# Two 256-column tiles in place of one 512-column tile, and other due times for the DMA transposes, in a planned attention and feed-forward kernel

## The chip, the core and the metric

The kernel runs on one core of a Trainium2 chip. A core has TensorE (PE, matrix multiplication into the PSUM banks), VectorE (DVE), ScalarE (ACT), GpSimd (POOL) and SyncE (SP, which here only issues DMAs), each with its own queue of instructions, and 16 DMA engines between HBM and the on-chip memory SBUF. The metric is the device time of one execution in microseconds. Smaller is better.

## What is computed

A decayed linear attention over 4 batches, 8 heads, 768 positions and 64 dimensions, in blocks of 64 positions, followed by a feed-forward layer with the gate h * cos(h):

```
for b in range(nb):
    intra = np.einsum('bhic,bhjc->bhij', qb, kb) * Dmask[None]
    intra = np.einsum('bhij,bhjd->bhid', intra, vb)
    inter = np.einsum('bhid,bhde->bhie', qb * lam_pow[None], kv_state)
    out[:, :, sl] = intra + inter
    kb_dec = kb * rev_pow[None]
    kv_state = lam_block[None, :, None, None] * kv_state + np.einsum('bhsd,bhse->bhde', kb_dec, vb)
...
x = attn_out.transpose(0, 2, 1, 3).reshape(B * S, H * D)      # 3072 x 512
h = x @ w_in                                                  # 3072 x 2048
g = h * np.cos(h)
return g @ w_out                                              # 3072 x 512
```

## The kernel before

**Blocks, pairs and tiles.** The 3072 rows are 24 blocks of 128 rows, numbered in the order in which they are worked. Two neighbouring blocks are a pair, one from each of two batches, and pair 2 to pair 11 go through `prepare`, `add_scores` and `add_stretch` (pairs 0 and 1, the lead-in, have their own code in `add_span`). The feed-forward layer works on tiles of blocks: the list `TILES` (line 21) says how many blocks each tile has, and `add_ffn(i)` emits the work of tile i. A tile of 4 blocks has 512 columns and holds two pairs, a tile of 2 blocks has 256 columns and holds one.

**One pair of attention.** SP loads q, k and v (line 253). GpSimd scales and casts them (lines 329, 333, 337). From pair 3 on, two DMA transposes issued by SP (line 365) make `qkT` from `qk`; pair 2 is transposed on TensorE. TensorE then does the scores (`ps_s`, line 407) and the update of the running state (`ps_kv`, line 419), and for the pair before the values (`ps_o`, line 470) and the carried part (line 502). VectorE masks the scores (line 412) and adds up the state (line 425), ScalarE casts the state (line 430) and the attention's output into `xT` (line 510), which is the input of the feed-forward layer. Most of the time the values of pair p, the scores and update of pair p+1 and the carried part of pair p stand together in TensorE's queue, as one group of 128 small matmuls.

**One tile of feed-forward.** For each of 16 hidden steps f, TensorE does four matmuls as wide as the tile into a PSUM bank `ps_h` (line 732), ScalarE takes the cosine (line 738) and VectorE multiplies it with `ps_h` into `g` (line 744), which frees the bank. For each block of the tile, 16 matmuls of 512 columns (line 779, in four quarters of four) make `ps_f`; ScalarE copies it to SBUF as `o_sb` (line 793), and SP stores it (lines 800 and 802).

**What sets the order.** The order of each engine's queue is made ahead of time by a small list scheduler, `Planner.order` (lines 74 to 117): each task has an engine, a duration, dependencies and a priority, PSUM banks and buffers are counted, and whichever task can start first on an engine goes next, ties by priority. The priorities of attention and of projections come from the tile lists `unit` and `begins` (lines 234 and 235), which come from `TILES`. `T_LAT` (line 28) tells the planner, for each pair, how many microseconds after the DMA transpose its result counts as there (line 372); a pair without an entry has 1.2. The planner's times only make the order; on the chip the engines wait on semaphores. `HELD` (line 29) makes the stores of the first twelve blocks wait until the transposes of pair 10 have been issued (line 808); their outputs lie in 12 buffers `o_held` until then, the later ones in 3 buffers `o_sb`. `ALONE` (line 27) names the pairs whose scores stand alone.

**Buffers that tie one pair or tile to another.** Eight PSUM banks in all. Three buffers each of `qk` and `qkT`, six of `v_s` (three pairs), two of `xT` and two of `g`: the attention of tile i writes the `xT` that the hidden steps of tile i-2 have read, and the gates of tile i write the `g` that the projections of tile i-2 have read.

Of the kernel before, what the change touches and what calls it, by code (L numbers as in the profile page):

```python
# [17 lines left out]

SPANS = 2
DMA_FROM = 6  # L20
TILES = [4, 2, 2, 2, 2, 4, 4, 4]
SPLIT = 5
BANKS = 8
LAG = 2
ATT = 0.95
LOAD_US = 1.22
ALONE = [3, 4]
T_LAT = {3: 2.46, 4: 4.62, 5: 3.15, 6: 4.42, 7: 3.9, 8: 3.84, 9: 6.24, 10: 5.52, 11: 4.89}
HELD = (10,) * 12

APART = [3, 11]
# [115 lines left out]
def kernel(  # L147
# [19 lines left out]
    KF = D_FF // P  # L167
    assert sum(TILES) == NBLK
    first = [sum(TILES[:i]) for i in range(len(TILES) + 1)]

# [62 lines left out]

    unit = [MM(n * P, 4 * KF) + MM(DM, KF * n) + ATT * n for n in TILES]
    begins = [sum(unit[:i]) for i in range(len(unit) + 1)]

    def prio_attn(n, part):
        i = next(i for i in range(len(TILES)) if n < first[i + 1])
        return begins[i - 1] + unit[i - 1] * (n - n % 2 - first[i] + 2 * part) / TILES[i]

# [71 lines left out]
    def tile_of(n):  # L312
        return next((i, n - first[i]) for i in range(len(TILES)) if n < first[i + 1])

    def prepare(pr):
# [51 lines left out]
        for i, src in enumerate((a, k_)):  # L367
            get = None if i else "qkT"
            if 2 * pr >= DMA_FROM:
                head, T[pr, i] = dma("SP", 1.4, 1.3, partial(transposes_dma, i=i), 2 * pr + i - LAG + 1.5,  # L370
                                     src + ([qkT_head[pr]] if i else []), get=get, ordered=False)
                T[pr, i].lat = T_LAT.get(pr, 1.2)
                if i and 2 * pr + LAG < NBLK:
# [563 lines left out]
```

## Time and profile before

| what | value |
|---|---|
| median of 3 runs | 202.32 us (202.25 to 202.38) |
| the profiled execution's own time | 202.32 us |
| its span, first to last instruction | 200.6 us |
| granted TensorE clock in every stretch | 1.00 |
| ps_h, 128x512, 236 matmuls | mean 379 ns of one |
| ps_h, 128x256, 296 matmuls | mean 273 ns of one |
| ps_f, 128x512, 368 matmuls | mean 379 ns of one |
| cosine on ScalarE, 128x512 and 128x256 | 687 and 478 ns |
| gate on VectorE, 128x512 and 128x256 | 690 and 423 ns |
| weight load for ps_h | 98 ns |
| mask of scores, sum of state on VectorE | 684 and 680 ns |
| copy of ps_f to SBUF on ScalarE | 587 ns |
| DMA transpose, issue to landing | 2.9 to 6.3 us, median 4.4 |

The duration of one matmul in the table includes its way through the array, and the next one starts before it ends; what a matmul takes of TensorE's time is the distance from its start to the next start. TensorE's work from about 14 us to 198 us of the span is the stretch that the change lies in: lead-in up to 43 us, then ten pairs of attention among seven tiles of feed-forward, and the closing projections.

### The profile page before, as it was taken

What the parts mean: (1) busy time and instruction counts of PE and PEld (TensorE: products, weight loads), DVE (VectorE), ACT (ScalarE), POOL (GpSimd) and SP (SyncE); (2) the same over time, 40 slices, a digit from 0 to 9 for tenths busy, and PEclk for the clock granted to TensorE, in tenths of its full rate; (3) what the DMA queues carried; (4) which work ended last, traced back from release to release, by engine and by line L of the source; (5) the groups of instructions that cost most, each with busy time, mean ns of one, the idle gap of its engine ahead of it and who ended that gap; (6) DMA issues with size and microseconds to landing.
All of it is one profiled execution on the core that took longest, in us unless ns stands there. A gap on an engine that the chain in (4) does not pass through costs nothing.

```text
span 200.6 us, 5756 instructions
## 1 busy us (share of the span) xinstructions
PE 195.4 (97%) x2407; PEld 110.2 (55%) x2407; DVE 111.8 (56%) x211; ACT 116.3 (58%) x221; POOL 64.7 (32%) x85
## 2 busy tenths in 40 slices
PE   8799999999999999999999999999999999999994
PEld 2467444547758647867655454544445444444443
DVE  2978772258957816966735679367445454444001
ACT  5878771139768636948654878377455564345120
POOL 5793003066462636372736364003700000000000
DMA  5999999989997999999999899898921010111112
GB/s 161 305 191 204 203 199 215 174 197 227 218 213 172 198 222 199 216 204 187 220 192 242 154 226 178 232 394 197 260 83 51 6 52 3 52 52 52 52 56 105
DMA packets 96620, 33.93 MB, mean 169 GB/s; under 512 B 84690, under 2 KB 93650, under 8 KB 96594
## 3 DMA queue, kind: packets, MB, share of 16 engines
q1 hardware_dynamic: 89088, 28.78, 65.1%
q0 software_dynamic: 7360, 4.72, 16.5%
q8 instruction: 19, 0.31, 0.6%
q10 hardware_dynamic: 146, 0.07, 0.1%
q14 instruction: 7, 0.06, 0.1%
HBM read 27.26 MB, written 6.29 MB: 167 GB/s over the span
## 4 chain that ended last, share of the span: by engine, by line
PE 85%; DMA 9%; SPq 2%; DVE 1%; POOL 1%; ACT 0%; issue 0%; POOLq 0%
PE ps_h L732 41%; PE ps_f L779 36%; DMA v_f<-in_v_dram 4%; DMA sp_f<-in_k_dram 3%; SPq L253 2%; DMA k_f<-in_k_dram 2%; PE ps_o L470 2%; PE ps_o L502 2%; PE ps_kv L419 1%; PE ps_s L407 1%; PE ps_o L638 1%; PE ps_kv L625 1%; POOL k_sp L593 1%; DVE v_s L337 0%; PE ps_t L601 0%
## 5 line engine op out<-in xcount | busy, mean ns | idle before, releaser
L744 DVE TENSOR_TENSOR g<-ps_h,cos 128x256 bf16<-128x256 f32 (+1 forms) x133 | 70.4, 542 | 39.5 <-ACT cos L738 38.3
L779 PE MATMUL ps_f<-w_out_sb,g 128*128 128x512 bf16 (+2 forms) x400 | 90.5, 371 | 0.0
L732 PE MATMUL ps_h<-xT,w_in_sb 128*128 128x256 bf16 (+1 forms) x532 | 89.5, 320 | 0.0
L738 ACT ACTIVATE cos<-ps_h,halfpi 128x256 f32<-128x256 f32 (+1 forms) x133 | 72.1, 571 | 27.6 <-PE ps_h L732 26.3
L732 PEld LDWEIGHTS <-w_in_sb 128*128 128x128 bf16 x532 | 51.5, 98 | 32.9 <-DVE xT L510 0.4
L779 PEld LDWEIGHTS <-g 128*128 128x128 bf16 x400 | 37.5, 98 | 40.4
L329 POOL TENSOR_TENSOR qk<-q_f,q_scale 128x512 bf16<-128x512 f32 x19 | 19.5, 1045 | 38.1 <-DMA q_f<-in_q_dram 31.5
L793 ACT COPY o_sb<-ps_f 128x512 f32<-128x512 f32 (+1 forms) x24 | 13.8, 573 | 24.5 <-PE ps_f L779 24.4
L337 POOL TENSOR_TENSOR v_s<-v_f,v_scale 128x512 bf16<-128x512 f32 x19 | 19.7, 1044 | 10.5 <-DMA v_f<-in_v_dram 10.1
L510 ACT CAST xT<-ps_o 128x512 bf16<-128x512 f32 x15 | 8.1, 588 | 11.5 <-PE ps_o L502 9.1
L412 DVE TENSOR_TENSOR s_m<-ps_s,mask 128x512 bf16<-128x512 f32 x20 | 12.9, 684 | 3.3 <-PE ps_s L407 2.8
L333 POOL CAST qk<-k_f 128x512 bf16<-128x512 f32 x18 | 11.1, 614 | 6.2 <-DMA k_f<-in_k_dram 6.1
L425 DVE TENSOR_TENSOR sum<-sum,ps_kv 128x512 f32<-128x512 f32 x15 | 10.2, 680 | 0.6
L430 ACT CAST S<-sum 128x512 bf16<-128x512 f32 x15 | 9.1, 616 | 2.3 <-DVE sum L425 2.2
L487 DVE COPY spare<-ps_o 1x1 f32<-1x1 f32 x8 | 1.2, 156 | 15.3 <-PE ps_o L470 15.3
L253 POOL DMA_DIRECT2D w_out_sb<-in_moe_w_out_dram x4 | 3.0, 776 | 15.8 <-DMA q_f<-in_q_dram 15.8
L793 DVE COPY o_sb<-ps_f 128x384 f32<-128x384 f32 x1 | 0.6, 556 | 11.5 <-PE ps_f L779 11.5
L470 PEld LDWEIGHTS <-v_s 64*64 64x64 bf16 x320 | 4.2, 106 | 4.6 <-issue 3.2
L470 PE MATMUL ps_o<-s_m,v_s 64*64 64x64 bf16 x288 | 5.9, 197 | 0.1
L617 DVE TENSOR_TENSOR s_m_sp<-ps_s,mask_sp 128x512 bf16<-128x512 f32 x8 | 5.1, 682 | 1.3 <-PE ps_s L612 1.3
L864 PE MATMUL ps_idle<-const-float32-1.0 128*128 128x512 f32 (+1 forms) x6 | 4.8, 893 | 0.8 <-PEq L921 0.8
L502 PE MATMUL ps_o<-qkT,S 64*64 64x64 bf16 x304 | 5.1, 195 | 0.0
(75 smaller groups left out, 83.6 us busy)
## 6 DMA issues: line engine op xcount, KB each, us to landing
q_f<-in_q_dram SPq DMA_DIRECT2D x20, 256.0 KB, 3.8
k_f<-in_k_dram SPq DMA_DIRECT2D x20, 256.0 KB, 4.5
v_f<-in_v_dram SPq DMA_DIRECT2D x20, 256.0 KB, 4.8
out_dram<-o_sb SPq DMA_DIRECT2D x19, 256.0 KB, 2.8
w_out_sb<-in_moe_w_out_dram POOLq DMA_DIRECT2D x4, 512.0 KB, 12.4
sp_f<-in_q_dram SPq DMA_DIRECT2D x2, 512.0 KB, 5.0
sp_f<-in_k_dram SPq DMA_DIRECT2D x2, 512.0 KB, 5.5
w_in_sb<-in_moe_w_in_dram POOLq DMA_DIRECT2D x2, 512.0 KB, 8.8
```

Source lines behind the costliest of these rows:

```text
L329: vec[e].tensor_mul(new_qk()[:, 0, :, s], live.pop(("q_f", 2 * pr + s)), q_scale[:, c, :].unsqueeze(2).to_broadcast([P, H, D]))
L333: (nc.scalar.copy if early else nc.gpsimd.tensor_copy)(new_qk()[:, 1, :, s], live.pop(("k_f", 2 * pr + s)))
L337: vec[e].tensor_mul(live["v_s", 2 * pr + s], live.pop(("v_f", 2 * pr + s)), v_scale[:, c, :].unsqueeze(2).to_broadcast([P, H, D]))
L412: nc.vector.tensor_mul(t, live["s", pr][s], mask.unsqueeze(1).to_broadcast([P, H, D]))
L425: nc.vector.tensor_add(new, live["sum", pr, 0] if half else live["sum", pr - 1, 1], live["kv", pr][half])
L470: yield lambda h=h: nc.tensor.matmul(o[halves[h % 2], h // 2], lhsT=live["v_s", n0 + s][m, h, :], rhs=live["s_m", n0 + s][m, h, :], start= ...
L502: nc.tensor.matmul(live["o", n0 + s][halves[h % 2], h // 2, halves[half]], lhsT=S[r, h, :], rhs=live["qkT", pr][r, 0, h, halves[half]], st ...
L732: nc.tensor.matmul(t[:, :n], lhsT=w_in_sb[:, kd, f * P:(f + 1) * P], rhs=live["xT", i][:, kd, at], start=(kd == 0), stop=(kd == KD - 1))
L738: nc.scalar.activation(c[:, :n], live["h", i, f, at.start][:, :n], AF.Sin, bias=halfpi)
L744: return nc.vector.tensor_mul(live["g", i][:, f, at], live.pop(("h", i, f, at.start))[:, :n], live.pop(("c", i, f, at.start))[:, :n])
L779: nc.tensor.matmul(live["f", i, j, piece][:, :width], lhsT=live["g", i][:, f, j * P:(j + 1) * P], rhs=w_out_sb[:, f, part], start=(f == 0) ...
L793: (nc.scalar.copy if eng == "ACT" else nc.vector.tensor_copy)(o[:, :width], live["f", i, j, piece][:, :width])
```

## The change

Two lists of constants change, and with them the order that the planner makes:

```diff
-TILES = [4, 2, 2, 2, 2, 4, 4, 4]
+TILES = [4, 2, 2, 2, 2, 2, 2, 4, 4]
...
-T_LAT = {3: 2.46, 4: 4.62, 5: 3.15, 6: 4.42, 7: 3.9, 8: 3.84, 9: 6.24, 10: 5.52, 11: 4.89}
+T_LAT = {3: 2.6, 4: 5.0, 5: 3.15, 6: 5.8, 7: 5.52, 8: 7.8, 9: 6.8, 10: 6.0, 11: 5.3}
```

Pairs 6 and 7, blocks 12 to 15, were one tile of four blocks and are two tiles of two. The planner now takes the results of the DMA transposes as there later, for all pairs but 3 (0.14 us later) and 5 (the same) by 0.4 to 4.0 us. No other line differs.

What follows for the instructions: the hidden steps of pairs 6 and 7 are 2 x 16 steps of four 256-column matmuls, with as many cosines and gates, in place of 16 steps of four 512-column matmuls. Around the end of tile 2 and from there on, TensorE's queue has attention and feed-forward in another order:

```
before (matmuls in order, from the hidden steps of tile 1 on)
ps_h 64 | scores 3, update 3 | ps_f 16 | values 3, carried 3 | ps_f 8 | ps_h 48 | ps_f 4 | scores 4, update 4 | ...
after
ps_h 64 | ps_f 4 | scores 3, update 3 | ps_f 16 | values 3, carried 3 | ps_f 12 | ps_h 44 | scores 4, update 4 | ...
```

The groups with the values of pairs 7 and 9 had projections right behind them, that of pair 8 hidden steps of 512 columns. Now each of the three has 256-column hidden steps right behind it: after the group of pair 7, two hidden steps, a quarter projection, two hidden steps, a quarter projection, and so on; after the groups of pairs 8 and 9, one hidden step, a quarter projection, two hidden steps. In the queues of ScalarE and VectorE the cosines, gates, casts and copies follow the same order. GpSimd's queue is unchanged. In SP's queue the stores of blocks 4 to 13 (before: 4 to 12) stand between the transposes of pair 10 and the loads of pair 11, and the store of block 14 stands between the two transposes of pair 11 (before: the store of block 13 stood ahead of both).

## The prediction

> **What bounds the kernel now.** I read the page's shares and slices first, then TensorE's own waits, then the chain that ended last in order of time, and last the timelines around one attention group and of SP's queue.
>
> ```profile
> span 200.6 us, 5756 instructions
> ...
> PE 195.4 (97%) x2407; PEld 110.2 (55%) x2407; DVE 111.8 (56%) x211; ACT 116.3 (58%) x221; POOL 64.7 (32%) x85
> ...
> PE   8799999999999999999999999999999999999994
> ```
>
> TensorE is busy 97% of the span and every slice but the first two and the last is full. The page warns that such a share is modelled, so the waits are needed too. TensorE's list of waits for other engines is short, and all of it lies in the lead-in:
>
> ```profile
> PE ps_idle L864 <- PEq L921: 0.8, 1, 0.8
> PE ps_t L601 <- DVE q_sp L593: 0.5, 1, 0.5
> PE ps_t L601 <- DVE k_sp L593: 0.3, 1, 0.3
> PE ps_t L601 <- POOL k_sp L593: 0.3, 1, 0.3
> ```
>
> The chain in order of time (start us, us, what) tells whether the matmuls follow each other at their own pitch:
>
> ```profile
> 46.36 7.02 PE ps_h L732 x64
> ...
> 77.85 6.99 PE ps_h L732 x64
> ...
> 109.76 9.50 PE ps_h L732 x44
> ...
> 120.24 0.45 PE ps_o L502 x32
> 120.69 4.42 PE ps_h L732 x20
> ...
> 183.89 13.87 PE ps_f L779 x80
> ```
>
> The first two rows are 64 matmuls of 256 columns: 7.02/64 = 109.7 ns and 6.99/64 = 109.2 ns each. The third is of 512 columns: 9.50/44 = 215.9 ns. The last is the closing projection without a break. I went through the start of every ps_h and ps_f matmul from 14.3 us on: apart from the step to another kind of matmul (0.09 us, once at each attention group), the one start that is late is at 42.8 us, by about 0.18 us, for v_s of pair 2. So from 43 us to the last matmul the order of TensorE's queue costs nothing but its work.
>
> **The change part by part.** The order of instructions of the two kernels differs on TensorE only after the 64 ps_h of tile 1, at 53.3 us of this trace; the lead-in, the 0.18 us and all of POOL's order are the same.
>
> *The split tile.* Pairs 6 and 7 were one tile of 512 columns; now each is a tile of 256. 16 hidden steps x 4 = 64 matmuls of 512 columns go, 128 of 256 columns come. 64 x (2 x 109.2 - 215.9) ns = 64 x 2.5 = +0.16 us on TensorE, in the path. With 109.7 it is 64 x 3.5 = +0.22; with the medians of start to start in the trace (109 and 216) it is 64 x 2 = +0.13. I take 0.16, the row of the undisturbed run of tile 3. The 64 more weight loads of 98 ns (6.3 us of weight-load time) lie under matmuls: in those same runs each 98 ns load is already hidden inside a 109 ns pitch; uncovered they would be up to 6.3 us, but 282 pairs of such matmuls in this trace keep a mean of 109.3 ns.
>
> The projections (ps_f) stay 128 wide in their weights and 512 in columns: none added. Attention groups stay: 11 stretches of small matmuls from 53 us on, in both orders, so the 0.09 us steps stay, 0.
>
> [...]
>
> *Cosine and gate.* By the page's groups of one form each, ScalarE does 32 cosines of 478 ns for 16 of 687 (+4.3 us) and VectorE 32 gates of 423 ns for 16 of 690 (+2.5 us), spread over the about 30 us in which pairs 6 and 7 are worked. ScalarE is busy 13.2 of the 20 us from 100 to 120 us and VectorE 11.2, and TensorE covers it: 0. In a run of hidden steps TensorE takes 4 x 109 = 437 ns for each; 14 cosines in a row took 5.71 us, 408 ns each, so ScalarE keeps up.
>
> *The due times (T_LAT) and the moved attention.* They only shift where attention stands among the feed-forward matmuls. Summing pitches over the new order from 53.31 us, the scores of pairs 3 to 11, at 53.3, 66.2, 74.9, 86.6, 96.3, 106.7, 119.3, 129.5 and 153.4 us now, come at about 54.2, 66.6, 74.9, 88.4, 98.1, 111.0, 121.6, 130.1 and 155.3. The trace has the second transpose of each pair landed at 52.2, 62.7, 72.3, 82.7, 93.7, 103.5, 114.1, 125.1 and 146.6. The least margin rises from 1.1 us (pair 3) to 2.0; none shrinks. Later attention frees qkT, qk and v_s later; three pairs of each are held, and the tightest, the transpose of pair 10 issued at 118.9, needs carried values of pair 7, which end at about 112.3. Loads are not delayed: 0.
>
> *SP's queue.* One more store (block 13) goes ahead of pair 11's loads, and one store (block 14) between its two transposes.
>
> ```profile
> 122.08 6.04 SPq L800 DMA_DIRECT2D out_dram<-o_sb  x8
> 128.21 5.72 SPq L802 DMA_DIRECT2D out_dram<-o_sb  x9
> 133.99 1.35 SPq L253 DMA_DIRECT2D q_f<-in_q_dram  x2
> ...
> 141.73 2.75 SPq L365 DMA_TRANSPOSE qkT<-qk  x2
> ```
>
> A store's issue is 5.72/9 = 0.64 us. Block 13's projection ends at about 132.7 in the new order, its copy (0.59 us) at about 133.6, before SP comes to it at 134.0; so pair 11's loads start 0.6 us later. Block 14's copy is done at about 143.1; SP waits there under 1 us with the transpose of k, and then only stores, behind it. It lands by about 148.5; the scores that want it come at 155.3. Cover: 6.8 us; 0.
>
> Sum: +0.16 us, bounds +0.13 and +0.22 without a stall. Span 200.6 + 0.16 = 200.8 us. The profiled execution's own time is 202.32, the same as the median of the three runs, with 1.7 us around the span; so 202.32 + 0.16 = **202.48 us**. Under 0.2% (0.40 us), about what a measurement of this kernel can tell from no change.
>
> **The rivals.**
>
> *Bank waits after the moved attention: slower, 203.2 us.* In the new order the groups of pairs 7/8, 8/9 and 9/10 are followed at once by 256-column hidden steps, which ask for a PSUM bank every 0.44 us, where the group at 119.25 us asks every 0.86. Each group takes 6 of 8 banks and VectorE frees four of them with two masks (684 ns) and two sums (680 ns). For it: the group's VectorE work ends late, here 5.4 us after its start:
>
> ```profile
> 119.18 0.32 PE L470 MATMUL ps_o<-s_m,v_s 64*64 64x64 bf16 x16
> ...
> 120.95 1.28 DVE L412 TENSOR_TENSOR s_m<-ps_s,mask 128x512 bf16<-128x512 f32 x2
> ...
> 122.15 0.68 DVE L425 TENSOR_TENSOR sum<-sum,ps_kv 128x512 f32<-128x512 f32 x1
> ```
>
> Against it: in spite of that, the chain shows 20 ps_h right behind at 4.42 us (221 ns each, the 0.09 us step in it), and the new order puts one or two hidden steps, then 0.86 us of projection, then two. Where VectorE starts the masks 0.66 us into a group, as at 86.49 us (87.15), the first bank is free at 1.35 us, just as the group's 1.34 us end, and the second at 1.95 against a need at 1.78 when no other bank is free. One group then costs between nothing and a mask, 0.68 us. One mask late at one group: 202.48 + 0.68 = 203.16; at all three, 204.5. It decides from a total of 0.24 us on.
>
> *Pair 11 late through SP: slower, 203.0 us.* It needs the 6.8 us of cover gone. The longest landing of a transpose here is 6.3 us against the median of 4.4, which takes 1.9 of it. The store ahead of the transpose of k would have to wait 5 us longer than worked out, a whole half of a block's projections and hidden steps; each microsecond beyond is one of TensorE's, and 0.5 of it gives 203.0.
>
> *The new order closes gaps: faster, down to 201.5.* For it speaks only the step at attention groups: were it hidden at all 11 (11 x 0.09 = 1.0 us), 202.48 - 1.0 = 201.5. Against it: the groups are as many, and the step stands at every one of them whatever its neighbours; other gaps there are none behind 53 us.
>
> *The change does nothing.* The orders differ, so only a cancelling gain could make it so; its time, 202.3, lies in the same 0.2%.
>
> **How the numbers follow.** Forecast, no stall, 202.40 to 202.60: 0.70. Bank waits: 0.22, of which 0.02 stay under 0.24 us. Pair 11: 0.04. Gaps closed: 0.04. So faster 0.04, same 0.70 + 0.02 = 0.72, slower 0.20 + 0.04 = 0.24. Range: from 202.30, the forecast's lower bound of 202.45 less the runs' own spread (202.25 to 202.38), to 203.20, one mask late; what lies beyond is several masks late and the gain.
>
> **What would show it.** TensorE's list of waits should again hold the lead-in alone; 128x256 ps_h should rise by 128 and 128x512 fall by 64, at 109 and 216 ns a start; 32 cosines more of 128x256. Scores of pair 8 near 111 us. A ps_h that waits for VectorE's masks or sums between 111 and 133 us would show the first rival; scores of pair 11 behind a transpose that lands after 155 the second. What would make it wrong is VectorE behind by more than one mask at those groups.

## The result, and the profile after

The changed kernel is slower. Its median is 203.46 us (202.75 to 205.34, 22 runs), that of the kernel before beside it 202.37 us (22 runs): a ratio of 1.0055, interval 1.0036 to 1.0074, so 0.55% or 1.1 us. The forecast was 202.48 us, no measurable change, with a range up to 203.20. The profiled execution took 203.63 us, with a span of 201.9 us (before: 202.32 and 200.6); the granted clock is 1.00 throughout.

The page of the changed kernel, shares of the span and the line on the instruction queue that will matter below (packets, MB, share of 16 engines):

```profile
span 201.9 us, 5935 instructions
...
PE 196.7 (97%) x2471; PEld 117.0 (58%) x2471; DVE 114.2 (57%) x227; ACT 118.4 (59%) x237; POOL 64.9 (32%) x85
...
q8 instruction: 19, 0.31, 0.6%
```

The reader is to see that TensorE has its 64 more matmuls (2471 for 2407), VectorE and ScalarE 16 more instructions each, and that TensorE is still busy for 97%. Busy time rose by 1.3 us, but the page's busy time is modelled; the waits say more. TensorE's list of waits in the changed kernel (us in total, times, longest):

```profile
PE ps_idle L864 <- PEq L921: 0.8, 1, 0.8
PE ps_h L732 <- issue: 0.8, 1, 0.8
PE ps_s L612 <- ACT kT_sp L604: 0.3, 1, 0.3
PE ps_t L601 <- DVE q_sp L593: 0.2, 1, 0.2
```

Three of the four rows are the lead-in, as before. The second is new: one matmul of ps_h is 0.8 us late, and its releaser is "issue", the profile's word for no releaser at all. Behind the lead-in no row names VectorE, a PSUM bank or a DMA. The chain in order of time (start us, us, what) shows where it is:

```profile
46.29 7.02 PE ps_h L732 x64
...
77.78 6.99 PE ps_h L732 x64
...
110.99 0.25 PE ps_o L470 x16
111.24 0.26 PE ps_s L407 x32
111.50 0.32 PE ps_kv L419 x32
111.82 0.16 PE ps_o L470 x16
111.98 0.35 PE ps_o L502 x32
112.32 0.98 PE ps_h L732 x8
113.30 0.86 PE ps_f L779 x4
114.17 0.77 PE ps_h L732 x7
114.93 0.79 issue
115.72 0.27 PE ps_h L732
115.99 0.86 PE ps_f L779 x4
...
185.16 13.87 PE ps_f L779 x80
```

The rows of 64 matmuls have the pitch of before (7.02 and 6.99 us), and so has the closing projection (13.87). The group of pairs 7 and 8 stands at 111 us and has its two hidden steps right behind it, eight matmuls, a quarter projection, and then seven matmuls of eight: between the seventh and the eighth, the last of one accumulation, 0.79 us pass. From start to start it is 1065 ns, where 109 is the pitch. The timeline of the changed kernel around it (start us, us, engine, line, operation, tiles, shape, and in brackets the idle time before it):

```profile
111.58 1.29 DVE L412 TENSOR_TENSOR s_m<-ps_s,mask 128x512 bf16<-128x512 f32 x2
...
112.25 1.05 PE L732 MATMUL ps_h<-xT,w_in_sb 128*128 128x256 bf16 x8
...
112.79 1.47 DVE L425 TENSOR_TENSOR sum<-sum,ps_kv 128x512 f32<-128x512 f32 x2
...
113.37 2.85 SPq L253 DMA_DIRECT2D v_f<-in_v_dram  x2
...
114.00 0.93 PE L732 MATMUL ps_h<-xT,w_in_sb 128*128 128x256 bf16 x7
...
115.72 0.27 PE L732 MATMUL ps_h<-xT,w_in_sb 128*128 128x256 bf16 x1 [0.79 <-issue]
115.72 0.64 PEld L779 LDWEIGHTS <-g 128*128 128x128 bf16 x4 [0.97 <-issue]
```

VectorE's masks and sums behind the group are over at 114.26 us and none of the matmuls waited for them. The eighth matmul uses the same bank as the three before it, an `xT` whose casts ended at 100.37 us, and weights of which the last load was issued at 13.8 us (the longest of them took 9.9 us to land). Weight loads and matmuls stop together, for 0.97 and 0.79 us, both down to "issue": it is TensorE's queue of instructions itself that stands still.

**What the span's 1.3 us are made of** (201.9 less 200.6, to the tenth of the page; 1.36 from the start of tile 1's hidden steps to the end, 155.60 for 154.24, and -0.07 in front of it): the pitch of the split tile, 128 x 109.3 - 64 x 215.9 ns = +0.17; the hole, 1065 - 109 ns = +0.96; the eleven attention groups, +0.22 in all (11.94 for 11.72 us, from the first small matmul of each to the next wide one; single starts in them are some 0.1 us late). That makes 1.35 of the 1.36.

### The profile page after: what moved, and what is told of

The parts are those of the page before. It is cut to its first block, busy times and chain, and to the rows that moved or that the text cites. A ratio compares the mean times of both kernels' runs of the same rounds, so it can differ in the third digit from the quotient of the medians.

```text
span 201.9 us, 5935 instructions
## 1 busy us (share of the span) xinstructions
PE 196.7 (97%) x2471; PEld 117.0 (58%) x2471; DVE 114.2 (57%) x227; ACT 118.4 (59%) x237; POOL 64.9 (32%) x85
## 4 chain that ended last, share of the span: by engine, by line
PE 90%; DMA 6%; SPq 1%; POOL 1%; issue 1%; ACT 0%; POOLq 0%
PE ps_f L779 42%; PE ps_h L732 41%; DMA sp_f<-in_k_dram 3%; DMA w_in_sb<-in_moe_w_in_dram 3%; PE ps_o L470 2%; PE ps_o L502 2%; PE ps_kv L419 1%; PE ps_s L407 1%; SPq L253 1%; POOL k_sp L593 1%; PE ps_t L359 0%; PE ps_kv L697 0%; PE ps_x L470 0%; ACT o_sb L793 0%; POOLq L593 0%
## 5 line engine op out<-in xcount | busy, mean ns | idle before, releaser
L744 DVE TENSOR_TENSOR g<-ps_h,cos 128x256 bf16<-128x256 f32 (+1 forms) x149 | 72.5, 501 | 44.0 <-ACT cos L738 42.8
L738 ACT ACTIVATE cos<-ps_h,halfpi 128x256 f32<-128x256 f32 (+1 forms) x149 | 75.3, 540 | 29.6 <-PE ps_h L732 29.3
L732 PE MATMUL ps_h<-xT,w_in_sb 128*128 128x256 bf16 (+1 forms) x596 | 91.2, 303 | 0.9 <-issue 0.8
L779 PE MATMUL ps_f<-w_out_sb,g 128*128 128x512 bf16 (+2 forms) x400 | 91.5, 371 | 0.0
L732 PEld LDWEIGHTS <-w_in_sb 128*128 128x128 bf16 x596 | 57.6, 98 | 30.1 <-DMA w_in_sb<-in_moe_w_in_dram 0.5
L329 POOL TENSOR_TENSOR qk<-q_f,q_scale 128x512 bf16<-128x512 f32 x19 | 20.0, 1065 | 43.8 <-DMA q_f<-in_q_dram 43.8
L793 ACT COPY o_sb<-ps_f 128x512 f32<-128x512 f32 (+1 forms) x24 | 13.8, 573 | 26.0 <-PE ps_f L779 26.0
```

What stands on the lines that cost most here:

```text
L329: vec[e].tensor_mul(new_qk()[:, 0, :, s], live.pop(("q_f", 2 * pr + s)), q_scale[:, c, :].unsqueeze(2).to_broadcast([P, H, D]))
L732: nc.tensor.matmul(t[:, :n], lhsT=w_in_sb[:, kd, f * P:(f + 1) * P], rhs=live["xT", i][:, kd, at], start=(kd == 0), stop=(kd == KD - 1))
L738: nc.scalar.activation(c[:, :n], live["h", i, f, at.start][:, :n], AF.Sin, bias=halfpi)
L744: return nc.vector.tensor_mul(live["g", i][:, f, at], live.pop(("h", i, f, at.start))[:, :n], live.pop(("c", i, f, at.start))[:, :n])
L779: nc.tensor.matmul(live["f", i, j, piece][:, :width], lhsT=live["g", i][:, f, j * P:(j + 1) * P], rhs=w_out_sb[:, f, part], start=(f == 0) ...
L793: (nc.scalar.copy if eng == "ACT" else nc.vector.tensor_copy)(o[:, :width], live["f", i, j, piece][:, :width])
```

## The experiments

**Theories.** *Instruction fetch:* TensorE's instructions come in blocks by DMA, and in the new order TensorE reaches the end of a block before the next one is there. For it: the hole has no releaser; the packets of the instruction queue number 19 in both kernels, of 16 KB each (16384 bytes in both traces), and TensorE's some 4,950 instructions (2471 matmuls and as many weight loads) are 19 blocks of about 256. In the order of the program the late matmul is the 3254th instruction. (TensorE's records in the trace, waits included, make it the 3266th; in every profile below that has a late start at a numbered instruction, the two counts differ by the same 12.) *Rival:* a wait on data, a bank or a due time after the moved attention, wherever the instructions lie.

### The two halves of the change, each alone

```diff
 e1_tiles_only          (after, with the due times of before)
-T_LAT = {3: 2.6, 4: 5.0, 5: 3.15, 6: 5.8, 7: 5.52, 8: 7.8, 9: 6.8, 10: 6.0, 11: 5.3}
+T_LAT = {3: 2.46, 4: 4.62, 5: 3.15, 6: 4.42, 7: 3.9, 8: 3.84, 9: 6.24, 10: 5.52, 11: 4.89}
 e2_due_times_only      (after, with the tiles of before)
-TILES = [4, 2, 2, 2, 2, 2, 2, 4, 4]
+TILES = [4, 2, 2, 2, 2, 4, 4, 4]
```

> The changed list of tiles with the due times of before. Theory F (fetch): the single hole in the changed kernel's profile, 0.85 us at 114.9 us between two matmuls of one accumulation and with no other engine named, is TensorE waiting for its own next instructions, and comes from small matmuls and 256-column steps standing close together; this kernel has the same tiles, and its group of pair 7/8 is followed by 256-column steps too, so it should lie 0.4 to 1.3 us above before, with a hole of the same kind. Theory D (due times): the due times alone moved the attention to a bad place; then this kernel costs only the extra width, +0.16 us, 202.4 to 202.6.

> The changed due times with the tiles of before. Theory F: groups are followed by 512-column steps, the queue is used up more slowly, so no hole: within 0.3 us of before. Theory D: about +0.9 us, the whole cost of the change less the extra width.

The tiles alone: 202.60 us (202.23 to 203.76, 12 runs) against 202.42, a ratio of 1.0009 [0.9997, 1.0021], 0.2 us as the pitch says. That is the time which the rival gave (202.4 to 202.6), and not the 0.4 to 1.3 us of the fetch. The profiled execution has a late start all the same, and smaller: at 114.86 us, 0.31 us late, again at instruction 3254, though that is another place of the feed-forward work.

The due times alone: 203.69 us (203.53 to 204.98, 6 runs), 1.0071 [1.0051, 1.0091]. So this half costs 1.3 us with the old tiles, but for another reason than the whole change does. Its chain in order of time:

```profile
101.48 6.91 PE ps_f L779 x32
108.39 0.25 PE ps_o L470 x16
...
109.37 0.44 PE ps_o L502 x32
109.81 1.07 ACT xT L510 x2
110.88 0.04 issue
110.92 7.07 PE ps_h L732 x32
```

Here TensorE runs out of other work: the tile of pairs 6 and 7 can't start its hidden steps before pair 7's `xT` is cast, and pair 7 was moved late. TensorE waits 1.1 us for ScalarE (its list of waits says 1.2). In the whole change tile and pair are one, pair 6's hidden steps need no pair 7, and this wait is gone. Neither theory had this cause; the fetch was wrong in its number, the rival near in the number only. The costs of the two halves don't add up, and neither one alone explains the whole: 0.2 and 1.3 us alone, 1.1 together.

### Shifting the instructions against the block boundaries

Small pairs of a weight load and a 16-column matmul, put into the lead-in before the second idle matmul, move every later instruction by twice their number; by the theory of the fetch the boundaries of the blocks stay where they are counted.

```diff
 e5_after_plus64: 32 pairs; e6_after_plus128: 64; e7_after_plus192: 96; e8_before_plus128: 64, in the kernel before
+    [nc.tensor.matmul(idle_ps[:16, :16], lhsT=nc.const_aps.tensor(1.0, [P, 16], BF16), rhs=nc.const_aps.tensor(1.0, [P, 16], BF16), start=True, stop=True) for _ in range(32)]
     ones_of(4 * P, F32)
 e11_after_swap32, e12_after_swap64: the 32 or 64 pairs in place of that idle matmul
```

> The changed kernel with 32 pairs of a weight load and a 16-column matmul on constants put into TensorE's queue in the lead-in, between 3 and 6 us, where TensorE waits for loads anyway: 64 instructions more, no work in the way of anything later. Theory F: instructions come in blocks of 256, so the ends of blocks now fall 64 instructions earlier in the rest of the queue; the hole at the 3254th instruction moves or goes, and the time changes by 0.3 us or more against the changed kernel (203.46). Worst place here: a block of 256 that is nearly the group of pair 9/10 alone, up to 3 us at 132 us if the fetch has no lead. Rival B or any cause tied to the place in the computation: the hole stays behind the group of pair 7/8, 203.2 to 203.8 us.

> The same with 64 pairs, 128 instructions. Theory F: no hole behind the group of pair 7/8, whose block now ends inside it after a long stretch; a hole as large as the present one can come behind the group of pair 8/9, about 126 us, whose block now begins 34 instructions into it as the present one does. 202.5 to 203.6 us. A cause tied to the place: 203.2 to 203.8, hole at 115 us.

> The same with 96 pairs, 192 instructions. Theory F: blocks begin 98, 226 and 130 instructions into the groups of pairs 7/8, 8/9 and 9/10, each with a long stretch of wide matmuls in it; no hole, 202.4 to 202.8 us. A cause tied to the place: 203.2 to 203.8, hole at 115 us. If the added pairs themselves cost time in the lead-in, the start of tile 1 (46.3 us) shows how much.

> The kernel before with 128 instructions more in the lead-in. Theory F: the kernel before has no hole because its groups are followed by 512-column steps or by projections, which use up half as many instructions in a microsecond, so the place of the blocks matters little: within 0.4 us of before. If it rises by more, before owes its time to where its blocks happen to end as well. Rival: within 0.2 us.

> The changed kernel with the second of the two wide idle matmuls of the lead-in (1.9 us) replaced by 32 pairs of weight load and 16-column matmul (27 ns each in the runs with added pairs, 0.9 us): 63 instructions more in the queue and no later start. Theory F: the block that ends behind the group of pair 7/8 begins ahead of it, no hole over 0.2 us at 115; from tile 1 to the end 154.9 us as with 64 added, so 202.6 to 203.0. A cause tied to the place: 203.2 to 203.8.

> The same with 64 pairs (1.75 us): 127 instructions more. Theory F: the hole stands at the 3766th instruction of the queue, at about 126 us, as it did with 128 added, and not at 115: 0.6 to 1.0 us, total 203.2 to 203.8 us, the changed kernel's own time from another place. A cause tied to the place: hole at 115 us.

The pairs had a price of their own that was set too low or left out: they hold the lead-in up by 0.6 to 1.6 us in the profiled executions (tile 1 starts at 46.87 to 47.89 us in place of 46.29 and 46.36). The medians are therefore no test: 203.36, 204.24, 204.32 and 203.21 us for e5 to e8 (ratios to before 1.0052 [1.0038, 1.0066], 1.0089 [1.0072, 1.0107], 1.0098 [1.0081, 1.0116], 1.0040 [1.0026, 1.0054]), 203.40 and 203.83 for e11 and e12 (1.0049 [1.0030, 1.0069], 1.0071 [1.0048, 1.0093]). What can be read is the place of the hole, and the time from the start of tile 1 to the end of the span:

```
kernel                  tile 1 to end, us   late start of TensorE
before                  154.24              none
after                   155.60              0.96 us at instruction 3254, 115.7 us
e5  after, +64          154.86              none
e6  after, +128         155.44              0.92 us at instruction 3766 = 3254 + 2 x 256, 127.3 us
e7  after, +192         154.60              none
e8  before, +128        154.73              0.24 us at instruction 4534 = 3254 + 5 x 256
e11 after, +63          154.79              none
e12 after, +127         154.68              none
```

The hole leaves the matmul at 115 us as soon as that matmul isn't the first of a block, with all data, banks, due times and the order of the matmuls unchanged. In e6 it comes back 12 us later, again at the first instruction of a block, in the middle of four matmuls of a projection; in after, whose order this is, the same four start at 126.06 us and their `g` were made by 105.89. TensorE's waits and its timeline in e6:

```profile
PE ps_f L779 <- issue: 0.8, 1, 0.8
```

```profile
125.90 0.59 PE L779 MATMUL ps_f<-w_out_sb,g 128*128 128x512 bf16 x2
127.25 0.59 PE L779 MATMUL ps_f<-w_out_sb,g 128*128 128x512 bf16 x2 [0.75 <-issue]
```

Against a simple reading: e12 has the same shift as e6 within a few instructions and no hole in its profiled execution. So the place is fixed by the block, but whether it is late, and by how much, differs from one kernel (or execution) to another. That part of e12's expectation was missed; the packets below show what differed. And the kernel before isn't free of this: shifted by 128 (e8), its stretch takes 0.49 us more, 0.24 of it one late start, where at most 0.4 us in all had been expected.

### What the fetch waits for

The trace has the packets of the instruction queue with their times. Beside the order of the program they give, worked out from the trace:

```
kernel  block that TensorE is in   fetch of the next block   first instruction of that block
before  2998, from 107.03          109.48 to 110.44          119.25, on time
before  3254, from 119.25          117.28 to 118.24          121.92, on time
after   2998, from 111.10          113.49 to 114.43          115.72, 0.96 late
e1      2998, from 109.73          112.67 to 113.63          114.86, 0.31 late
e4      2998, from 111.00          112.00 to 113.31          114.73, on time
```

There is one fetch a block: in before and in after 18 packets for the 18 blocks that begin at instructions 438 to 4790, and a 19th behind them. While TensorE is in a block, the next one is fetched; the packet of the one after that started, at the earliest, when TensorE had about 40 instructions of its block left (22 matmuls with their weight loads in before, packet at 165.71 us, and 21 in after, at 181.02; 15 in the second row). Where TensorE is held up, it starts again 1.29 us (after) and 1.23 us (e1) behind the end of the packet. All the traces say the same: they hold 328 blocks with their packets, and no block started less than 1.23 us behind the end of its packet. The six late starts of after, e1, e6, e8, e9 and e20 (the last two come below) are the six that start nearest to it, 1.23 to 1.40 us. So a late start is a block whose packet came just too late for TensorE, and e12 escapes because its packet starts 1.13 us into the block at 122.6 us, where e6's starts 2.29 us in. The changed order makes a block short: the group of 128 small matmuls is 256 instructions in 1.33 us, as many as a whole block, and 256-column hidden steps use two instructions each 109 ns. Without the hole, TensorE crosses block 2998 in 3.7 us (111.00 to 114.73 in e4). In the kernel before, the group is followed by projections and hidden steps of 512 columns, two instructions each 216 ns, and that block takes 12.2 us; its fetch starts as late, 2.45 us into the block, and costs nothing. Where a block of before is short (3254, 2.68 us), the fetch of the block behind it had started 2 us before TensorE entered it.

The next question is why the fetch of after starts 2.4 us into the block. The DMA engines are full of pair 10's loads then (windows of the changed kernel; the last three columns are the granted clock, the DMA share and GB/s; the share adds up the packets' times over 16 engines and can pass 1):

```profile
110.00:112.00 2.00, 2.00 (x122) 1.34 (x121) 1.42 (x4) 0.64 (x2) 0.94 (x1) 1.00 0.73 157
112.00:113.50 1.50, 1.50 (x40) 1.20 (x28) 1.47 (x3) 1.10 (x3) 0.00 (x0) 1.00 1.24 284
```

The four kernels below test it with loads of longer runs. They load q, k and v of the pairs as 128 runs of 2 KB each in place of 1024 of 256 bytes.

```diff
-            i = start(nc.sync, t, src[b, :, c * P:(c + 1) * P, :].transpose([1, 0, 2]), deps)
+            i = start(nc.sync, t, src[b].rearrange("h s d -> (h s) d")[c * P * H:(c + 1) * P * H].rearrange("(p k) d -> p k d", k=H), deps)
 e3_before_long_runs, e4_after_long_runs: all these loads; e9_long_runs_pair10: with n // 2 == 10 alone, in after; e10_long_runs_but_pair10: all but those, in after
```

> The kernel before, with each load of q, k and v of pairs 2 to 11 reading 128 runs of 2 KB in place of 1024 runs of 256 bytes (the same bytes, other rows, so the attention is of other data). Its order on TensorE is that of before. It is the base for the next run: within 0.4 us of before, since before has no hole; a little less if the wait for v_s at 42.8 us (0.18 us) goes.

> The changed kernel with the same longer runs. Theory F: the fetch of instructions stands behind the loads on the DMA engines; with a quarter of the packets gone from them it comes in time, and this kernel is 0.1 to 0.4 us above the one before with long runs. Rival B (bank waits on VectorE in executions that were not profiled): loads don't matter, it stays 0.9 to 1.3 us above.

> The changed kernel with the loads of pair 10 alone (q, k, v; on SP from 110.1 to 116.2 us, around the hole) in runs of 2 KB, other rows of the inputs; all other loads as they are. Theory F with the loads of that moment in the way: the fetch that was served at 113.5 us comes earlier, the hole goes or is under 0.3 us, 202.5 to 202.9 us. If the fetch is late for another reason (all traffic together, the chip's memory), the hole stays: 203.2 to 203.8.

> The counterpart: every load but pair 10's in runs of 2 KB. Theory F with the loads of that moment in the way: the hole stays, 203.0 to 203.7 us less what long runs gave the kernel before (0.3). If it is the traffic in general: 202.3 to 202.6, as with long runs everywhere (202.36).

With long runs in all these loads the changed kernel takes 202.36 us (201.96 to 202.60, 11 runs; 0.9991 [0.9979, 1.0003] of before) and the kernel before 202.05 (201.80 to 203.01, 11 runs; 0.9987 [0.9976, 0.9999]). The difference between the two is 0.31 us where it was 1.1, and the stretch at 115 us runs through:

```profile
112.22 1.05 PE L732 MATMUL ps_h<-xT,w_in_sb 128*128 128x256 bf16 x8
113.10 1.03 PE L779 MATMUL ps_f<-w_out_sb,g 128*128 128x512 bf16 x4
113.96 1.04 PE L732 MATMUL ps_h<-xT,w_in_sb 128*128 128x256 bf16 x8
114.84 1.03 PE L779 MATMUL ps_f<-w_out_sb,g 128*128 128x512 bf16 x4
```

e9 and e10 were to say which loads matter, and both came out against what the theory of the fetch had expected of them. With pair 10's loads in long runs, e9's hole should have gone; it takes 203.82 us (203.17 to 204.23, 6 runs; 1.0059 [1.0038, 1.0080]) and has it, 1.02 us at instruction 3254 (TensorE's waits):

```profile
PE ps_h L732 <- issue: 0.9, 1, 0.9
```

With all others in long runs and pair 10's as they were, e10 should have kept it; it takes 202.41 (202.08 to 204.02, 12 runs; 1.0009 [0.9991, 1.0027]) and has none. Its windows say why:

```profile
110.00:112.00 2.00, 2.00 (x124) 1.34 (x124) 1.45 (x4) 0.61 (x2) 0.49 (x1) 1.00 0.74 167
112.00:113.50 1.50, 1.50 (x36) 1.17 (x27) 1.44 (x3) 1.12 (x3) 1.34 (x2) 1.00 0.00 0
```

In e10 all that stands ahead of pair 10's loads is done sooner, so SP issues them from 103.32 to 108.81 us and not, as in after, from 110.07 to 116.22, and from about 111.7 to 113.5 us no load is under way: a DMA share of 0.00 (a packet counts where it starts, so the instruction packet itself isn't in this window) where after has 1.24. The fetch starts at 111.97 us. In e9 what stands ahead of pair 10's loads is as in after, so they come at that moment, in long runs, and it starts at 113.98. So by these runs it isn't the length of the runs but whether transfers are under way when the block is wanted. In e4 and e10, the engines idle (in e4 a share of 0.04 from 110 to 112 us and 0.00 to 113.5), it starts 1.0 us after TensorE enters the block; in after it is 2.4 us. From 46 us on in all the traces: in the 33 blocks with idle engines (a DMA share under 0.05 from 0.7 us behind TensorE's entry to the fetch), 31 fetches start by 1.15 us and the last at 1.56; in the 147 with a share above 0.5 the median is 1.7 us and the longest 3.45. The delay is not fixed by the loads alone: e12's fetch, above, started after 1.13 us and e6's after 2.29, with the same loads in the same order.

The last four kernels leave the way of loading and the lead-in as they are. The DMA transposes are replaced by plain copies, and then the first projections are split in two 256-column halves, which adds 64 (e19) or 128 (e20) instructions long before the stretch at 110 us:

```diff
 e17_before_copy, e18_after_copy
-            return nc.sync.dma_start_transpose(out=new_T()[:, i], in_=...)
+            return nc.sync.dma_start(out=new_T()[:, i].rearrange("t h s -> t (h s)"), in_=...)
 e19_after_copy_split2, e20_after_copy_split4: e18, and for the projections of the first two or four blocks
-                            nc.tensor.matmul(live["f", i, j, piece][:, :width], lhsT=..., rhs=w_out_sb[:, f, part], start=(f == 0), ...)
+                            for a, z in ([(0, 256), (256, 512)] if 4 * i + j < 4 else [(0, width)]):
+                                nc.tensor.matmul(live["f", i, j, piece][:, a:z], lhsT=..., rhs=w_out_sb[:, f, part][:, a:z], start=(f == 0 and a == 0), ...)
```

> The kernel before with each DMA transpose replaced by a plain copy of the same 256 KB within SBUF (q and k of pairs 3 to 11 stay untransposed, so the attention is of other data). TensorE's queue is that of before. Base for the next three: 201.9 to 202.5 us; transposes end earlier, nothing on TensorE changes.

> The changed kernel with plain copies in place of the transposes. If the transposes' traffic is what stands ahead of the late fetch, the hole goes: 0.1 to 0.4 us above the base. If the loads are, it stays: 0.7 to 1.3 us above.

> The same with the 32 projections of the first two blocks (at 29 to 37 us) made as two matmuls of 256 columns each: the same sums, 64 instructions more from there on, 32 x 2.6 ns = 0.08 us more of TensorE, the lead-in untouched. Theory F: the end of a block comes 64 instructions earlier, inside the group of pair 7/8, and the stretch ahead of it is long; no hole behind that group: 0.2 to 0.5 us above the base, whatever the run before shows. A cause tied to the place in the computation: the time of the run before + 0.1 us.

> The same for the first four blocks: 128 instructions, +0.17 us. Theory F: a block begins 34 instructions into the group of pair 8/9, as the changed kernel's does in that of pair 7/8; a hole, if any, at the 3766th instruction near 126 us; 0.3 to 1.3 us above the base. A cause tied to the place: the time of the run without splits + 0.2 us.

e17 takes 202.17 us (201.91 to 203.07, 12 runs; 0.9991 [0.9975, 1.0008]), e18 202.41 (202.16 to 203.71, 12 runs; 1.0005 [0.9991, 1.0019]): the change costs 0.24 us here, and e18 has no hole; its fetch starts at 112.02. By e18's expectation this speaks for the transposes' traffic, but the run can't single it out: here too SP is done with pair 10's loads by 107.02 us, and from 112.0 to 113.5 us the DMA share is 0.04, which is the instruction packet itself (16 KB, 11 GB/s), so loads and transposes are both gone from that moment. With no hole in e18 there is none for a shift to remove, so e19 (202.38, 202.03 to 203.74, 12 runs; 1.0005 [0.9984, 1.0026]) tells nothing apart. e20 takes 202.86 (202.68 to 203.85, 7 runs; 1.0041 [1.0025, 1.0056]), 0.45 us above e18 (a cause tied to the place would have given 0.2) for 0.17 us of work (64 matmuls of 512 columns split: 64 x 2.7 ns). In its profiled execution one matmul is 0.17 us late, at 125.56 us, and it is instruction 3766, the first of a block that TensorE reaches 4.0 us after the one before. So a kernel with an untouched lead-in gets a late start back, at the place that the fetch gave, when its instructions are shifted; it is a small one, and the DMA traffic around it was not held fixed.

**What is shown and what is not.** Shown: six late starts of 0.17 to 1.02 us (after, e1, e6, e8, e9, e20), all at instructions a multiple of 256 apart, and all 1.23 to 1.40 us behind the end of the packet that brought them, nearer than any other block; the hole gone in e4, e10 and e18, where no other DMA traffic stands around that packet (a DMA share of 0.00, 0.00 and 0.04 from 112.0 to 113.5 us). That the traffic delays the packet rests on these runs and on the comparison of blocks above; which transfers do it was not separated. From the start of tile 1 to the end, the changed kernel and its variants take 154.32 to 154.86 us where no start is late by over 0.2 us (e4 154.52, e10 154.51, e18 154.41, e19 154.32, e20 154.55, and the four in the table), 154.98 with 0.31 us (e1) and 155.44 to 155.87 with 0.9 us and more (e6, after, e9 155.87). The two small ones, in e8 and e20, weigh less: late starts of 0.05 to 0.2 us inside attention groups stand at other instructions too, also in kernels without a hole (0.14 us at 111.37 us in e4), and e8's lies in such a group. e20's lies in a projection: from 48 us on, no wide matmul right behind another one is late by over 0.04 us in any of the eighteen traces, except the holes of after, e1, e6 and e9 and this one.

Open: when TensorE asks for a block, since only the packet is on record; what the small late starts inside the groups are, some 0.1 to 0.2 us of what the change still costs without the hole; how large the hole is in executions that weren't profiled (the lowest of after's 22 runs, 202.75 us, is still 0.4 above before's median, of which 0.17 is work); and why e12's packet started earlier than e6's. No version here beats the kernel before as it stands: e3's gain of 0.13% comes with other rows loaded.

## Why the prediction was wrong

- *The split tile, +0.16 us.* Right. In the trace it is +0.17 (109.3 ns a start for 128, 215.9 for 64), and the change as a whole costs 0.31 (e4 to e3) and 0.24 us (e18 to e17) where the hole is gone, 0.2 in e1.
- *Cosine and gate, 0.* Right: no wait of TensorE for them.
- *The due times and the moved attention, 0.* The places of the scores were right up to the hole: 54.11, 66.55, 74.83, 88.3, 98.1 and 111.07 us, against 54.2, 66.6, 74.9, 88.4, 98.1 and 111.0; behind it 122.58, 131.08 and 156.24 stand 0.9 to 1.0 us behind the 121.6, 130.1 and 155.3 forecast, which is the hole. No transpose was late: TensorE's list of waits names none.
- *SP's queue, 0.* Right in its result; SP's issue of pair 11's loads began at 134.74 us (forecast 134.6), and the transposes were issued by 145.6, ten microseconds before the scores that want them:

```profile
126.93 7.76 SPq L802 DMA_DIRECT2D out_dram<-o_sb  x10
134.74 1.20 SPq L253 DMA_DIRECT2D q_f<-in_q_dram  x2
...
143.86 0.36 SPq L802 DMA_DIRECT2D out_dram<-o_sb  x1
144.32 1.31 SPq L365 DMA_TRANSPOSE qkT<-qk  x1
```

- *The attention groups, 0.* They cost +0.22 us (11.94 for 11.72). The prediction had gone through the starts of ps_h and ps_f matmuls alone; inside the groups single starts are late, in the old order too (the group at 119.18 us takes 1.44 us, that at 106.52 takes 1.33).
- *The rival with the bank waits* (0.22) gave 203.16 us, near what came, and the same place, right behind the moved group of pair 8. But it didn't happen: no matmul waited for VectorE's masks or sums. A right place and size with a wrong mechanism is luck; the test that the prediction named for it, a ps_h that waits for VectorE between 111 and 133 us, says no.
- **The step that failed** is in the bounds and the sum: "So from 43 us to the last matmul the order of TensorE's queue costs nothing but its work", carried over from the old order to the new, with bounds of "+0.13 and +0.22 without a stall". That was a fact of the old order, read from starts that were all on time. It doesn't hold for the new one, because the supply of TensorE's own instructions was taken to be without limit: a term put at nothing without a reason, which measured 0.96 us. What the old trace could have told was there: 19 instruction packets and their times, one of them 2.45 us into its block, and by its pitches that TensorE would cross 256 instructions at 111 us in some 3.7 us, where the group of the old order had 512-column matmuls behind it. Moving the densest stretch of instructions (a group of 128 small matmuls) next to the next densest (256-column steps), on top of loads that fill the DMA engines, was the change's real content.

The rows for this: packets of 16 KB, 256 instructions apart, fetched one ahead, with a hole of 0.96 us in after, 0.92 in e6 and 1.02 in e9. Had more been fetched ahead, a packet that starts 2.4 us into a block would have cost nothing.

## What to carry to other kernels

Before moving groups of very small matmuls, count instructions as well as work: take TensorE's time for each 256 instructions (matmul and weight load are two), and compare it with what a fetch took in these traces: about 1.0 us until it started (e4, e10), 0.95 us for the packet (0.94 to 0.96 in after, before and e1; 1.31 in e4) and 1.25 us until the block was used (1.29 in after, 1.23 in e1). That adds up to an estimate of 3.2 us with idle DMA engines; in after, where loads fill them, it was 4.6 us (111.10 to 115.72). A wait that the profile puts down to "issue", in the middle of an accumulation, with matmuls and weight loads stopped together, was the sign of it here (0.79 us in after, 0.75 in e6, 0.86 in e9); the proof was that the hole stayed with the instruction's number and not with the matmul (3254 in after, 3766 in e6). And when two constants change together, each alone can show a cost that the two together don't have (e2), so a half is no term of the sum.

## What the runs showed of the hardware

- TensorE's stream was fetched in 16 KB packets, one for 256 instructions, each 0.9 to 2.0 us (0.88 to 1.66 in before and after), on a DMA queue of its own (q8, 19 packets) that took 0.6% of the DMA engines' time and still held TensorE for 0.96 us in after. The packet of block 3254 started late while loads were under way (113.49 us in after, at a DMA share of 1.24, and 113.98 in e9) and early where none were (111.97 to 112.02 in e4, e10 and e18, at a share of 0.00 to 0.04), and in all the traces no block's first instruction started less than 1.23 us behind the end of its packet.
- Loads as 2-KB runs alone didn't bring the fetch forward: e9's starts 2.45 us into its block, as late as that of after (2.41).
- 64 small pairs of weight load and matmul, 26 ns each, put ahead of a place in the lead-in where TensorE of before waits 0.52 us (for `q_sp`, at 5.72 us), weren't free: they took 1.7 us (3.41 to 5.10 us) and the lead-in of before grew by 0.7 us (e8).
